# An mLSTM layer and a mixture of experts on one core: gate weights by another queue, all one-hot slot tables on VectorE, a wait before the second rank's weights, and a new order

## The chip, the cores and the metric

The kernel runs on one core of a Trainium2 chip. TensorE multiplies, VectorE, ScalarE and GpSimd work beside it, and SyncE issues most loads; every engine takes its instructions in the order in which the program was built and waits at the first whose inputs are not there. The metric is the device time of one launch in microseconds (us).

## The reference

Two layers follow each other. The first is a recurrence over 768 steps for 4 batches of 8 heads of 40 dimensions; the kernel computes it in closed form, row by row, as a numerator, a denominator and an output gate. The second sends each of the 3072 rows to the expert with the largest gate logit:

```python
h_tilde = np.einsum('bhde,bhe->bhd', C, qt)
y[:, :, t] = o * h_tilde / denom                  # first layer, x = y as 3072 rows of 320
logits = x @ w_gate
e_idx = np.argmax(logits, axis=1)
for e in range(E):                                # 8 experts
    h = np.maximum(x[e_idx == e] @ w1[e], 0.0)    # 320 -> 1024
    ye = h @ w2[e]                                # 1024 -> 320
    out[mask] = gate_w[mask, None] * eom[mask, e, None] * ye
```

## The kernel before, in words

**First stage.** The rows come in 24 tiles of 128, six per batch, worked in pairs n = 0 to 11 (three pairs per batch). For a pair, `hats_rows` (L1077) has TensorE make the numerators (L1007), ScalarE take the absolute denominator (L1095) and the sigmoid of the gate (L991), and VectorE multiply and divide (L1101, L1107, L1109). `logits_of` (L1164) transposes the rows (L1183, copies L1173), multiplies them with the gate weights `wg` (L488, L491), copies (L1195), transposes back (L1197) and adds (L1200). GpSimd then stores the pair to DRAM as part of `xn` (L1213).

**Routing.** Tiles are counted in five groups of 6, 6, 6, 4 and 2 (GROUPS, L35). `route` (L309) finds each row's expert and its place among the expert's rows, with VectorE and short products (L336 to L342). `invert` (L360) turns places into lists of row numbers: a one-hot table of slots `A`, 128 columns per tile, is multiplied with a table `T` (L388, L392, L398) and added to `acc` (L401). `A` is made in one of two ways: for a group in ONDVE (L50) by one VectorE compare over all its tiles (L373), else by two ScalarE activations per tile (L380, L382). Before, the groups of 4 and 2 tiles use VectorE, the three groups of 6 tiles use ScalarE.

**Early pair.** After groups 0 and 1 the busiest expert's first 256 rows among the first half are known. `early_gather` (L1228) has GpSimd fetch them in two indirect DMAs, after the row numbers `gi` (L414). `pair_products` (L694) transposes them (L741), splits them into a high and a low part (ScalarE L711, L713; VectorE L715, L717), multiplies with the expert's split first weights (64 products, L760), evacuates (L723, L725), and multiplies with its second weights (48 products, L776). The weights are split by L674 and L656. `first_gather` (L1240) and `first_columns` (L1251) fetch and transpose (L1272) the same expert's next 256 rows once all groups are known.

**Second stage.** The experts follow in order of size (rank 0 to 7): hidden products (L814, evacuated by L815 and L816), transposes of the next rank's rows (L788), result products (L841, evacuated by L849), scatters to the output (L679). `start` (L1397) issues the next rank's weight loads on SyncE's queue, `expert_load` (L583) and `gather` (L1401) its rows.

**What sets the order.** In the first stage no order stands in the code: the class `Play` (L100) holds each engine's clock, takes lines of work with weights and due times (tables at L41 to L78) and builds the instructions in the order that it finds; where TensorE would wait it puts in `fill` products (`warmup`, L1028), whose result nobody reads. SyncE's order is left to the framework.

Of the kernel before, what the change touches and what calls it, by code (L numbers as in the profile page):

```python
# [20 lines left out]
N, DM, E, F = B * S, H * D, 8, 1024  # L21
P = 128
# [15 lines left out]
GROUP1 = STARTS.index(TAKEN) - 1  # L38
TOP = 4096
TMAX = 32  # L40
WCHAIN, WSCALE, WPART, WPIECE, WEVAC, WGATE, WTOTAL, WLAST = -56800, 2000, -3800, -20600, 600, -12100, 3700, -30900  # L41
WSEND = -9800
WCAST, WGATHER, WSPLIT = 2000, -10000, -107800
AHATS, ALOGITS, AGATE = [-500, 21100, 8000, 3300, -11200, 12700, 3000, -11600, 10000, 11800, 9700, 3000], [600, -22800, -19800, -1600, -19600, -16300, -38600, 31500, -14300, -2800, -34800, 1200], [-11000, 11600, -11800, 10300, -5800, -1100, 13000, 14500, -8000, -1500, -2500, 12900]
AROUTED, ASEND, AREST = [4100, 0, 12300, 300, -1500], [-11800, -5300, -36700, 0, 0, 9900, 400, -8100, -15900, -7600, 22000, 19400], [6100, 3100, -3000, -7500, 5500, 900, 5800, -12000, 3000, -1100]
ASTATE, APAIRS = [27900, 3700, 300, 4100], [-800, -6000, -3300, 23700]
AKEYS = [0, 0, 0, 0]
AINV = [-400, -13500, -94300, -29100, -33500]
WSLOT, WINV, WFIRST = -1200, 1300, -10000
ONDVE = (3, 4)  # L50
STORE = 750
INVERTED = 3
QS = 1 << 12
WSTATE, WHATS, WLOGITS = -11900, -22200, -308100
SHORT = {'T': 1.0, 'V': 2.0, 'A': 3.0, 'G': 0.0}
AHEAD = 4
SCATTER = 1430
GATHERED = 2700
PERIOD, RISE, KEEP = 3413.3, 0.9, 0.7
FILL, SLACK, PART, NFILL = 120, 50, 0.85, 102  # L60
SEM = {"T": 52, "V": 35, "A": 36, "G": 200}
TAIL = {"T": 160, "V": 83, "A": 105, "G": 60}
LANDED = [
    ("small", (0, 14500, 21000, 27000)),
    ("queries", (9800, 18000, 24900, 32200, 13300)),
    ("load", (11000, 22300, 28300, 34700, 15400)),
]
SMALLS = (13500.0, 18500.0)
ROWS0 = 11500.0
WEIGHTS = (1400, 1400, 1350, 1800, 1800)  # L70
ISSUE, REACH, RINGFREE, MOVE = 1300, 1900, 30600, 1060
CLOCK = {"T": 9700.0, "V": 11500.0, "A": 10000.0, "G": 9200.0}
WPAIRS = -17800
WCHAIN1, WEARLY1 = -165400, 1550
SWITCH = 100
SEG = 8
FIRST = 3
WABS = -1700  # L78
FAR = 1 << 20
KW = [(0, 128), (128, 128), (256, 64)]  # L80
KL = [0, 128, 192]
# [127 lines left out]
def tile_mlstm_moe(  # L209
# [18 lines left out]
    nc = tc.nc  # L228
# [42 lines left out]
    wg = const.tile([P, 3, 32], F32, name="wg")  # L271
# [31 lines left out]
    def sync_after(inst, others):  # L303

        info = mybir.DependencyInfo(mybir.DependencyClass.Sync, mybir.DependencyReason.DATA)
        for o in others:
            tc.add_manual_dep(inst.ins, o.ins.name, info, reason="rows")
# [200 lines left out]
    G = rt.tile([BH, L0], F32, name="G")  # L508
# [71 lines left out]
        yield dve(8)  # L580
        nc.vector.tensor_copy(nr, ki)

    def expert_load(e_reg, twice=True):  # L583

        x = {}
        we = w1[bass.ds(e_reg, 1)].rearrange("a k f -> (a k) f")
        w2e = w2[bass.ds(e_reg, 1)].rearrange("a k f -> (a k) f")
        x["st1"], x["st2"] = [], []
        for kk in range(3):
            ws = wst.tile([P, F], F32, name="ws", bufs=3)  # L590
            if kk < 2:
                nc.sync.dma_start(ws, we[kk * P : (kk + 1) * P])
            else:
                for u in range(1 + twice):
                    nc.sync.dma_start(ws[64 * u : 64 * u + 64], we[256:320])
            x["st1"].append(ws)
        for u in range(2):
            ws = wst.tile([P, 4, DM], F32, name="ws2", bufs=2)
            nc.sync.dma_start(ws, w2e[u * 512 : (u + 1) * 512].rearrange("(c p) f -> p c f", p=P))
            x["st2"].append(ws)  # L600
        return x

    def expert_gather(pool, x, C, gi, src=xn, rows=N):

        n = (C + P - 1) // P
        x["ms"], x["C"] = [(j, min(P, C - j * P)) for j in range(n)], C
        width = src.shape[1]
        x["xg"] = xg = pool["xg"].tile([P, n, width], F32, name="xg")
        x["ids"] = gi if src is xn else xg[:, :, ID].bitcast(I32)
        for j, M in x["ms"]:  # L610
            yield "G", SCATTER
            nc.gpsimd.indirect_dma_start(  # L612
                out=xg[:, j, :] if src is xn else xg[:, j, :].bitcast(I32),
                out_offset=None,
                in_=src[:rows, :],
                in_offset=bass.IndirectOffsetOnAxis(ap=gi[:, j : j + 1], axis=0),
                bounds_check=rows - 1,
                oob_is_err=False,
            )
    def expert_weights(pool, x, cuts=1, rest=nc.vector):  # L620

        w1h = pool["w"].tile([P, 3, F], F32R, name="w1h")
        w1l = pool["w"].tile([P, 3, F], F32R, name="w1l")
        w2h = pool["w"].tile([P, F // P, DM], F32R, name="w2h")
        w2l = pool["w"].tile([P, F // P, DM], F32R, name="w2l")
        x["w"], x["parts"] = (w1h, w1l, w2h, w2l), 0
        for kk in range(3):
            for u in range(cuts):
                us = slice(u * F // cuts, (u + 1) * F // cuts)
                nc.scalar.copy(w1h[:, kk, us], x["st1"][kk][:, us])  # L630
                nc.vector.tensor_tensor(w1l[:, kk, us], x["st1"][kk][:, us], w1h[:, kk, us].bitcast(F32), ALU.subtract)  # L631
                x["parts"] += 1
                yield
        for u in range(2):
            for v in range(cuts):
                n = 4 // cuts
                vs = slice(v * n, v * n + n)
                us = slice(4 * u + v * n, 4 * u + v * n + n)
                nc.scalar.copy(w2h[:, us], x["st2"][u][:, vs])  # L639
                rest.tensor_tensor(w2l[:, us], x["st2"][u][:, vs], w2h[:, us].bitcast(F32), ALU.subtract)  # L640
                x["parts"] += 1
                yield
# [230 lines left out]
    with ExitStack() as actx:  # L873
# [53 lines left out]
        nc.scalar.dma_start(vab[:, 0:1], vp[:, 0:1])  # L927
        nc.scalar.dma_start(kt[L0:, 0:1], kn[:, 0:1, :DM])
        nc.scalar.dma_start(qkt[96:104, 0:1], qk0[96:104, 0:1])
        nc.sync.dma_start(kt[:L0, 0:1], kn[:, 0:1, :DM])  # L930
        lq = load_q(0, (L0, 2 * P, 4 * P, S))
        lo = load_o(0, (0, 2, 4, NCH))
# [101 lines left out]
        with tc.manual_schedule(engines=ENG):  # L1034
# [13 lines left out]
                eg.rearrange("p a b -> p (a b)")[:, L0:], G[:, L0 - 1 : L0].to_broadcast([BH, 2 * P - L0]), AF.Exp, scale=-1.0  # L1048
            )
            run(load_small(1))  # L1050
            nc.gpsimd.dma_start(wg[:, 0:2, : 2 * E], wgo[:, 0:2])
            nc.gpsimd.dma_start(wg[64:128, 2, : 2 * E], wgo[0:64, 2])
            wT_ps = psX.tile([P, BH], F32, name="wT_ps", tag="xt_ps")
            nc.tensor.transpose(wT_ps, wl.rearrange("p a b -> p (a b)"), ident[:BH, :BH])
            nc.vector.tensor_copy(wT, wT_ps)
# [18 lines left out]
            px, fx, apart, opened = {}, {}, [], []  # L1074
# [313 lines left out]
    with ExitStack() as mctx:  # L1388
# [5 lines left out]

        lt = mctx.enter_context(tc.tile_pool(name="lt", bufs=1))
        later = lt.tile([BH, 2, S - L0], F32, name="later")
        def start(r, x):  # L1397
            ev = nc.sync.value_load(er[0:1, r : r + 1], min_val=0, max_val=E - 1)
            x.update(expert_load(ev))

        def gather(r, x, gi=None):  # L1401
            if gi is None:
# [7 lines left out]
        with tc.manual_schedule(engines=ENG):  # L1410
            x, parts = {**fx, "w": px["w"]}, iter(())
            xs = {r: {"apart": apart} for r in range(1, E)}
            y = xs[1]
            start(1, y)
            run(gather(1, y, fx["next"]))
            for ob, j, M in px["leave"]:
                scatter(px, ob, j, M)
# [3 lines left out]
            for r in range(E):  # L1421
                if r + 1 < E:
                    y = xs[r + 1]
# [32 lines left out]
                x = y  # L1456
# [239 lines left out]
```

## Time and profile before

| | us |
|---|---|
| median of 3 runs | 278.29 |
| lowest, highest | 277.62, 279.69 |
| the profiled execution, its own time | 279.5 |
| its span | 277.7 |
| TensorE busy in the span | 264.1 (95%) |
| VectorE busy | 176.4 (64%) |
| ScalarE busy | 144.5 (52%) |
| GpSimd busy | 87.2 (31%) |

The profiled execution took 1.2 us more than the median of the runs. 1.8 us of its time lie outside its span. Busy time is an average over both stages; a stage is read from the windows, the timeline and the chain of waits.

### The profile page before, as it was taken

Reading aid. Unit: us, or ns where it says so; the run is one execution under the profiler, and the core shown is the slowest. Engines: PE = TensorE matmul, PEld = TensorE weight load, DVE = VectorE, ACT = ScalarE, POOL = GpSimd, SP = SyncE. Lnnn points to the kernel's source line nnn. Section 1 sums busy time; section 2 is a strip of 40 time slices with the busy share of each in tenths; the row PEclk is TensorE's granted clock in tenths of the full one; section 3 lists DMA queues with packets and bytes.
Section 4 is the critical chain, followed back from the end, with each engine's and each line's share of the span. In section 5 each row is a group of like instructions: output and inputs, shape, how many; then the busy total and the mean of one; then the engine's idle time right before and its main releaser. Section 6 shows DMA issues by size and latency. Waiting matters only on the chain.

```text
span 277.7 us, 5611 instructions
## 1 busy us (share of the span) xinstructions
PE 264.1 (95%) x2023; PEld 245.9 (89%) x2023; DVE 176.4 (64%) x526; ACT 144.5 (52%) x329; POOL 87.2 (31%) x109
## 2 busy tenths in 40 slices
PE   8979999899899999999999999999999999999990
PEld 5868888678789988999899989999999999899990
DVE  4544999799637986882885078608946955952300
ACT  4345677895517565633553266327626735732320
POOL 8251063353626116052403250323033231013021
PEclk9999999999999999999999999999999999999998
DMA  5999765971985587562555145524852761000000
GB/s 149 289 368 327 292 232 189 339 277 45 263 283 137 165 241 232 153 201 82 172 139 198 61 137 175 173 89 120 230 202 84 235 191 61 1 26 32 0 31 30
DMA packets 22355, 46.19 MB, mean 166 GB/s; under 512 B 2536, under 2 KB 15286, under 8 KB 22320
## 3 DMA queue, kind: packets, MB, share of 16 engines
q1 hardware_dynamic: 17856, 31.54, 36.9%
q0 software_dynamic: 4176, 14.04, 15.8%
q8 instruction: 18, 0.29, 0.4%
q10 hardware_dynamic: 288, 0.19, 0.3%
q14 instruction: 17, 0.14, 0.1%
HBM read 37.69 MB, written 8.42 MB: 166 GB/s over the span
## 4 chain that ended last, share of the span: by engine, by line
PE 53%; issue 17%; DMA 11%; DVE 8%; POOL 3%; SPq 2%; ACT 1%; POOLq 1%; DVEq 0%
PE hp L814 23%; PE op L841 22%; DMA xr<-in_on 7%; POOL out L679 3%; PE two L776 2%; DMA xg<-xn,gi 2%; PE xp L788 2%; DMA qTt<-in_qT 2%; SPq L912 1%; DVE xr L1101 1%; DVE w1l L656 1%; PE hat L1007 1%; POOLq L1455 1%; DVE xr L1109 1%; POOL xg L612 1%
## 5 line engine op out<-in xcount | busy, mean ns | idle before, releaser
L816 DVE SCALAR_TENSOR_TENSOR hl<-hp,hh 128x256 fp32r<-128x256 f32 (+6 forms) x64 | 35.6, 556 | 62.9 <-ACT hh L815 62.0
L679 POOL DMA_INDIRECT out<-ob,oi x28 | 31.6, 1127 | 117.4 <-ACT ob L849 101.5
L841 PE MATMUL op<-w2h,hh 128*128 128x320 f32 (+4 forms) x208 | 64.5, 311 | 0.0
L841 PE MATMUL op<-w2l,hh 128*128 128x320 f32 (+4 forms) x208 | 63.9, 308 | 0.0
L841 PE MATMUL op<-w2h,hl 128*128 128x320 f32 (+3 forms) x200 | 61.7, 309 | 0.0
L814 PE MATMUL hp<-xh,w1h 128*128 128x512 f32 (+6 forms) x168 | 58.0, 347 | 0.0
L814 PE MATMUL hp<-xh,w1l 128*128 128x512 f32 (+6 forms) x168 | 58.0, 347 | 0.0
L815 ACT ACTIVATE hh<-hp 128x256 fp32r<-128x256 f32 (+7 forms) x64 | 31.7, 495 | 33.4 <-PE hp L814 33.4
L814 PE MATMUL hp<-xl,w1h 128*128 128x512 f32 (+6 forms) x112 | 38.7, 346 | 0.0
L841 PEld LDWEIGHTS op<-w2h,hh 128*128 128x128 f32 (+4 forms) x208 | 37.9, 183 | 0.2
L612 POOL DMA_INDIRECT xg<-xn,gi x24 | 27.7, 1154 | 31.6 <-DVE w1l L631 9.2
L841 PEld LDWEIGHTS op<-w2l,hh 128*128 128x128 f32 (+4 forms) x208 | 37.5, 180 | 0.0
L841 PEld LDWEIGHTS op<-w2h,hl 128*128 128x128 f32 (+3 forms) x200 | 36.6, 183 | 0.0
L849 ACT ACTIVATE ob<-op,sc 128x320 f32<-128x320 f32 (+3 forms) x25 | 13.2, 526 | 43.7 <-PE op L841 43.7
L814 PEld LDWEIGHTS hp<-xh,w1l 128*128 128x128 f32 x168 | 31.6, 188 | 2.1
L814 PEld LDWEIGHTS hp<-xh,w1h 128*128 128x128 f32 x168 | 31.5, 188 | 2.0
L631 DVE TENSOR_TENSOR w1l<-ws,w1h 128x512 fp32r<-128x512 f32 x42 | 28.9, 687 | 0.0
L630 ACT CAST w1h<-ws 128x512 fp32r<-128x512 f32 x42 | 25.7, 613 | 0.0
L640 DVE TENSOR_TENSOR w2l<-ws,w2h 128x640 fp32r<-128x640 f32 x28 | 22.5, 823 | 0.9 <-ACT w2h L639 0.6
L814 PEld LDWEIGHTS hp<-xl,w1h 128*128 128x128 f32 x112 | 21.0, 188 | 1.4
L639 ACT CAST w2h<-ws 128x640 fp32r<-128x640 f32 x28 | 19.9, 716 | 0.0
L1007 PE MATMUL hat<-Cm,qTt 128*128 128x123 f32 (+3 forms) x144 | 18.9, 278 | 0.0
(238 smaller groups left out, 423.1 us busy)
## 6 DMA issues: line engine op xcount, KB each, us to landing
ws<-in_w SPq DMA_DIRECT2D x16, 640.0 KB, 4.9
ws<-in_w SPq DMA_DIRECT2D x16, 512.0 KB, 4.0
xn<-xr POOLq DMA_DIRECT2D x12, 336.0 KB, 3.7
ws<-in_w SPq DMA_DIRECT2D x15, 256.0 KB, 4.2
qTt<-in_qT SPq DMA_DIRECT2D x3, 1056.0 KB, 18.6
xr<-in_on SPq DMA_DIRECT2D x3, 960.0 KB, 17.5
xr<-in_on SPq DMA_DIRECT2D x3, 320.0 KB, 8.2
qTt<-in_qT SPq DMA_DIRECT2D x2, 384.0 KB, 8.7
```

The source lines that it names most:

```text
L612: nc.gpsimd.indirect_dma_start(out=xg[:, j, :] if src is xn else xg[:, j, :].bitcast(I32), out_offset=None, in_=src[:rows, :], in_offset=b ...
L630: nc.scalar.copy(w1h[:, kk, us], x["st1"][kk][:, us])
L631: nc.vector.tensor_tensor(w1l[:, kk, us], x["st1"][kk][:, us], w1h[:, kk, us].bitcast(F32), ALU.subtract)
L639: nc.scalar.copy(w2h[:, us], x["st2"][u][:, vs])
L640: rest.tensor_tensor(w2l[:, us], x["st2"][u][:, vs], w2h[:, us].bitcast(F32), ALU.subtract)
L679: i = nc.gpsimd.indirect_dma_start(out=out[:, :], out_offset=bass.IndirectOffsetOnAxis(ap=x["oi"][:M, j : j + 1], axis=0), in_=ob[:M, j, : ...
L814: nc.tensor.matmul(hp, a, c, start=(i == 0), stop=(i == len(mm) - 1))
L815: nc.scalar.activation(hh[:, f, :C], hp, AF.Relu)
L816: nc.vector.scalar_tensor_tensor(hl[:, f], hp[:, :C0], 0.0, hh[:, f, :C0].bitcast(F32), ALU.max, ALU.subtract)
L841: nc.tensor.matmul(op[:n], a, c, start=(i == 0), stop=(i == len(mm) - 1))
L849: nc.scalar.activation(ob[:M, j], op[:M], AF.Copy, scale=x["sc"][:M, j : j + 1])
L1007: nc.tensor.matmul(to, qTt[:, g, t0 : (c + 1) * P], Cm[b][:, cg], start=(g == 0), stop=(g == 2))
```

## The change

Four things are done, and the order tables are replaced by others:

1. The two loads of the gate weights `wg` go from GpSimd's queue (issued after the first batch's narrow loads) to ScalarE's queue at the start.
2. ONDVE holds all five groups: every one-hot table is one VectorE compare, of 768 columns for a group of 6 tiles, and the 36 ScalarE activations are gone.
3. The first weight load of the second rank waits for the two gathers of the first rank's rows (`after=fx["gathers"]`).
4. The narrow loads of batches 2 and 3 have later due times (SMALLS), with the landing times that `Play` reckons with, and its weights are new.

```diff
-WCHAIN, WSCALE, WPART, WPIECE, WEVAC, WGATE, WTOTAL, WLAST = -56800, 2000, -3800, -20600, 600, -12100, 3700, -30900
+WCHAIN, WSCALE, WPART, WPIECE, WEVAC, WGATE, WTOTAL, WLAST = -11600, 1500, -1800, -10100, -14800, -12700, 3700, -52300
...
-ONDVE = (3, 4)
+ONDVE = (0, 1, 2, 3, 4)
...
-GATHERED = 2700
+GATHERED = 3000
...
-    ("small", (0, 14500, 21000, 27000)),
+    ("small", (0, 14500, 22800, 30500)),
...
-SMALLS = (13500.0, 18500.0)
+SMALLS = (15500.0, 23500.0)
...
-    def expert_load(e_reg, twice=True):
+    def expert_load(e_reg, twice=True, after=()):
...
-                nc.sync.dma_start(ws, we[kk * P : (kk + 1) * P])
+                i = nc.sync.dma_start(ws, we[kk * P : (kk + 1) * P])
+                if after and not kk:
+                    sync_after(i, after)
...
-            nc.gpsimd.indirect_dma_start(
+            i = nc.gpsimd.indirect_dma_start(
...
+            x.setdefault("gathers", []).append(i)
...
+        nc.scalar.dma_start(wg[:, 0:2, : 2 * E], wgo[:, 0:2])
+        nc.scalar.dma_start(wg[64:128, 2, : 2 * E], wgo[0:64, 2])
...
-            nc.gpsimd.dma_start(wg[:, 0:2, : 2 * E], wgo[:, 0:2])
-            nc.gpsimd.dma_start(wg[64:128, 2, : 2 * E], wgo[0:64, 2])
...
-        def start(r, x):
+        def start(r, x, after=()):
...
-            x.update(expert_load(ev))
+            x.update(expert_load(ev, after=after))
...
-            start(1, y)
+            start(1, y, fx["gathers"])
```

The instruction rows below are the built programs'; the changed program's line numbers are higher by 2 from L593 on, by 3 from L620 on (L715 becomes L718), and by 5 between L930 and L1050.

ScalarE while groups 0 and 1 are inverted, before:

```order
L380 ACTIVATE far<-io_99,s_699 128x128
L1173 COPY xt<-xt_ps 128x3x128
L382 ACTIVATE A<-far 128x128
L1173 COPY xt<-xt_ps 128x3x128
L380 ACTIVATE far<-io_99,s_699 128x128
L382 ACTIVATE A<-far 128x128
L380 ACTIVATE far<-io_99,s_875 128x128
L1095 ACTIVATE dn<-hat 128x16
L382 ACTIVATE A<-far 128x128
L1195 COPY lt<-lg 128x128
```

and VectorE's rows for the same table of group 1 in the change:

```order
L364 TENSOR_SCALAR s_846<-rk 128x6
L367 SCALAR_TENSOR_TENSOR s_848<-s_846,rk 128x6
L388 TENSOR_TENSOR T<-block,s_846 128x192
L373 TENSOR_TENSOR A<-io_99,s_848 128x768
L502 COPY cnt<-ct 128x8
L392 TENSOR_TENSOR T<-T,number 128x192
```

ScalarE's slot activations stood between the copies (L1173, L1195) that the logits wait for; now VectorE has one wide compare instead.

VectorE ahead of the early pair's split (L715), before:

```order
L345 TENSOR_TENSOR t_1200<-pr,hots_135 128x16
L373 TENSOR_TENSOR A<-io_99,s_1190 128x512
L350 TENSOR_REDUCE rk<-t_1200 128x2
L392 TENSOR_TENSOR T<-T,number 128x128
L364 TENSOR_SCALAR s_1218<-rk 128x2
L656 TENSOR_TENSOR w1l<-ws,w1h 64x512
L367 SCALAR_TENSOR_TENSOR s_1230<-s_1218,rk 128x2
L502 COPY cnt<-ct 128x8
L388 TENSOR_TENSOR T<-block,s_1218 128x64
L572 TENSOR_TENSOR ns<-cnt,skip 128x8
L373 TENSOR_TENSOR A<-io_99,s_1230 128x256
L715 TENSOR_TENSOR xl<-two,xh 128x512
```

and in the change:

```order
L1203 TENSOR_REDUCE xr_216<-lg 128x2x16
L392 TENSOR_TENSOR T<-T,number 128x192
L315 TENSOR_REDUCE lmax<-xr_216 128x2
L323 TENSOR_REDUCE cm<-oh 128x4
L373 TENSOR_TENSOR A<-io_99,s_1073 128x768
L318 TENSOR_TENSOR oh<-xr_216,lmax 128x16
L326 TENSOR_TENSOR hots_134<-oh,cm 128x32
L437 TENSOR_REDUCE smax<-xg 128x2
L320 TENSOR_TENSOR oh<-oh,c_92 128x16
L718 TENSOR_TENSOR xl<-two,xh 128x512
L401 TENSOR_TENSOR acc<-acc,ix 128x32
```

The ranks and tables of the last two groups (4 and 2 tiles) stood ahead of the split, and stand behind it now.

TensorE where the first rank's rows are transposed (L1272), before, where 42 of the 48 of L776 stand behind the last row:

```order
L760 MATMUL two<-xh,w1l 128x256
L776 MATMUL two<-w2h,hh 128x320
L776 MATMUL two<-w2l,hh 128x320
L776 MATMUL two<-w2h,hl 128x320
L1272 MATMUL xp<-ident,xg 128x128 x2
L776 MATMUL two<-w2h,hh 128x320
L776 MATMUL two<-w2l,hh 128x320
L776 MATMUL two<-w2h,hl 128x320
L1272 MATMUL xp<-ident,xg 128x128 x2
```

and in the change, where 36 of L779 stand ahead of the first row:

```order
L779 MATMUL two<-w2h,hh 128x320
L779 MATMUL two<-w2l,hh 128x320
L779 MATMUL two<-w2h,hl 128x320
L1275 MATMUL xp<-ident,xg 128x128 x2
L779 MATMUL two<-w2h,hh 128x320
L779 MATMUL two<-w2l,hh 128x320
L779 MATMUL two<-w2h,hl 128x320
L1275 MATMUL xp<-ident,xg 128x128 x2
```

The transposes moved behind 39 of the 48 second products of the early pair, from behind 3 of them.

## Rows read from the trace of the kernel before

**Rows 1.** The page: engine, busy us, share of the span, instructions.
```profile
PE 264.1 (95%) x2023; PEld 245.9 (89%) x2023; DVE 176.4 (64%) x526; ACT 144.5 (52%) x329; POOL 87.2 (31%) x109
```
**Rows 2.** Windows of the second stage: length, busy time of each engine, clock, DMA.
```profile
100.00:150.00 50.00, 50.00 (x290) 45.88 (x289) 37.37 (x87) 26.46 (x53) 14.56 (x12) 1.00 0.56 170
200.00:250.00 50.00, 50.00 (x330) 49.27 (x329) 33.16 (x81) 26.99 (x58) 11.55 (x10) 1.00 0.37 116
```
**Rows 3.** The chain of waits: start, length, what; pieces from four places.
```profile
12.20 19.32 DMA xr<-in_on
...
67.23 6.09 DMA xg<-xn,gi
...
75.02 5.36 PE two L776 x36
...
82.33 6.89 PE hp L814 x56
```
**Rows 4.** Windows, VectorE alone: length, busy, instructions, clock, DMA share, GB/s.
```profile
25.47:62.99 37.52, 34.57 (x136) 1.00 0.77 269
50.00:53.40 3.40, 2.39 (x13) 1.00 1.02 331
20.00:25.47 5.47, 2.07 (x7) 1.00 1.03 311
```
**Rows 5.** Timeline of the handover: start, length, instruction, idle before and releaser.
```profile
62.32 0.67 DVE L715 TENSOR_TENSOR xl<-two,xh 128x512 fp32r<-128x512 f32 x1
...
62.92 0.17 DVE L401 TENSOR_TENSOR acc<-acc,ix 128x32 f32<-128x32 f32 x1
...
63.14 0.25 PE L398 MATMUL ix<-T,A 128*128 128x32 f16 x4 [0.19 <-DVE acc L401]
...
63.24 0.37 PE L760 MATMUL two<-xh,w1h 128*128 128x256 f32 x1
```
**Rows 6.** Groups of VectorE by form: busy us, mean ns, idle before.
```profile
L963 DVE TENSOR_TENSOR Pm<-sp,trif 128x256 f32<-128x256 f32 x4 | 1.7, 421 | 1.2 <-PE sp L958 1.2
...
L373 DVE TENSOR_TENSOR A<-io,s 128x512 f16<-128x512 f32 x1 | 0.7, 682 | 0.0
L373 DVE TENSOR_TENSOR A<-io,s 128x256 f16<-128x256 f32 x1 | 0.4, 409 | 0.0
L388 DVE TENSOR_TENSOR T<-block,s 128x128 f16<-128x128 int32 x1 | 0.3, 285 | 0.0
...
L320 DVE TENSOR_TENSOR oh<-oh,c 128x32 f32<-128x32 f32 x1 | 0.2, 182 | 0.0
```
**Rows 7.** Groups of ScalarE: the slot activations.
```profile
L380 ACT ACTIVATE far<-io,s 128x128 f32<-128x128 f32 x18 | 7.2, 400 | 0.0
L382 ACT ACTIVATE A<-far 128x128 f16<-128x128 f32 x18 | 5.6, 311 | 0.2
```
**Rows 8.** Timeline of the start: ScalarE's queue and first exponential, and TensorE's first logits.
```profile
2.35 0.72 ACTq L929 DMA_DIRECT2D qkt<-in_qk  x1
...
4.50 0.29 ACT L1045 ACTIVATE wl<-w 32x128 f32<-32x128 f32 x1
...
15.69 0.38 PE L488 MATMUL lg<-xt,wg 128*32 128x128 f32 x5 [1.75 <-DMA wg<-in_wgo]
```
**Rows 9.** Timeline of GpSimd: the early pair's gathers, the first rank's, the second's.
```profile
55.92 1.37 POOL L612 DMA_INDIRECT xg<-xn,gi  x1 [0.31 <-issue]
...
65.57 1.35 POOL L612 DMA_INDIRECT xg<-xn,gi  x1 [6.05 <-DVE ei L539]
67.23 1.03 POOL L612 DMA_INDIRECT xg<-xn,gi  x1 [0.30 <-DVE ki L579]
...
70.98 0.99 POOL L612 DMA_INDIRECT xg<-xn,next  x1 [0.31 <-issue]
```
**Rows 10.** Timeline of TensorE: three waits behind the start of the early pair.
```profile
67.72 0.39 PE L760 MATMUL two<-xh,w1h 128*128 128x256 f32 x1 [0.30 <-DVE hl L725]
...
73.37 0.33 PE L1272 MATMUL xp<-ident,xg 128*128 128x128 f32 x1 [1.02 <-DMA xg<-xn,gi]
...
82.33 0.39 PE L814 MATMUL hp<-fxh,w1h 128*128 128x256 f32 x1 [0.39 <-ACT ob L732]
```
**Rows 11.** All indirect gathers (L612), from issue to landing.
```profile
DMA to landing us min/median/max: 3.0/4.1/9.0
```
**Rows 12.** Timeline: the second rank's first weight loads, and their first cast.
```profile
67.79 0.96 SPq L592 DMA_DIRECT2D ws<-in_w  x2
...
86.35 0.61 ACT L630 CAST w1h<-ws 128x512 fp32r<-128x512 f32 x1
```

More of the change, by code (lines that the diff above doesn't have):

```diff
@@ L40 @@
 TMAX = 32
-WCHAIN, WSCALE, WPART, WPIECE, WEVAC, WGATE, WTOTAL, WLAST = -56800, 2000, -3800, -20600, 600, -12100, 3700, -30900
[L42 to L46, printed above, removed]
+WCHAIN, WSCALE, WPART, WPIECE, WEVAC, WGATE, WTOTAL, WLAST = -11600, 1500, -1800, -10100, -14800, -12700, 3700, -52300
+WSEND = -33700
+WCAST, WGATHER, WSPLIT = 2000, -69500, -16000
+AHATS, ALOGITS, AGATE = [10000, -2100, 8000, -1000, -5100, -15900, 300, 8600, 300, 500, 200, 0], [0, 300, 100, -42500, -5400, -4700, 0, -100, -600, 27200, 2900, -18600], [4100, -18600, 6500, -100, -16900, -10700, -4100, -3000, 4700, 15400, -4900, -8000]
+AROUTED, ASEND, AREST = [1800, -12000, -3100, -47400, -11000], [6000, 11000, 10500, 4100, -41200, 16700, 4900, 1200, 53800, -100, 0, 300], [-9500, 4200, -10700, 6000, -1000, -3100, 3000, 1900, -100, 300]
+ASTATE, APAIRS = [8000, 0, -5400, 11600], [21900, 300, -6400, 4700]
 AKEYS = [0, 0, 0, 0]
-AINV = [-400, -13500, -94300, -29100, -33500]
-WSLOT, WINV, WFIRST = -1200, 1300, -10000
-ONDVE = (3, 4)
+AINV = [-19200, -5200, 22600, -5900, -15500]
+WSLOT, WINV, WFIRST = -56100, -128600, -38000
+ONDVE = (0, 1, 2, 3, 4)
 STORE = 750
@@ L53 @@
 QS = 1 << 12
-WSTATE, WHATS, WLOGITS = -11900, -22200, -308100
+WSTATE, WHATS, WLOGITS = -41300, -22400, -328000
 SHORT = {'T': 1.0, 'V': 2.0, 'A': 3.0, 'G': 0.0}
@@ L63 @@
 LANDED = [
-    ("small", (0, 14500, 21000, 27000)),
-    ("queries", (9800, 18000, 24900, 32200, 13300)),
-    ("load", (11000, 22300, 28300, 34700, 15400)),
-]
-SMALLS = (13500.0, 18500.0)
-ROWS0 = 11500.0
+    ("small", (0, 14500, 22800, 30500)),
+    ("queries", (10400, 18500, 26000, 33000, 14300)),
+    ("load", (11900, 22900, 29700, 35500, 15900)),
+]
+SMALLS = (15500.0, 23500.0)
+ROWS0 = 11800.0
 WEIGHTS = (1400, 1400, 1350, 1800, 1800)
[L71 to L74, printed above, removed]
+ISSUE, REACH, RINGFREE, MOVE = 1300, 1900, 31800, 1060
+CLOCK = {"T": 10100.0, "V": 11700.0, "A": 10000.0, "G": 8200.0}
+WPAIRS = 2000
+WCHAIN1, WEARLY1 = -232000, 1550
 SWITCH = 100
@@ L77 @@
 FIRST = 3
-WABS = -1700
+WABS = -72900
 FAR = 1 << 20
```

## The prediction

> **What bounds the kernel now.** I read the page's totals first: TensorE is busy 95% of the span [rows 1]. The windows say where the other 5% can be: in the second stage TensorE is busy 50.00 of 50.00 us, twice [rows 2]. Nothing there can be won by this change, which leaves the second stage's products alone; a gain there would need fewer products. So the end comes a fixed stretch of TensorE work after the early pair's products begin (63.24 us [rows 5]), and the change is worth the shift of that moment, plus what is added to TensorE's work or waits behind it.
>
> What sets that moment is read backwards. The first product of the pair (L760) follows the last slot products (L398), which waited for VectorE's L401, and VectorE had just finished the split L715, at 62.99 [rows 5]. VectorE is the engine to look at: between the numerators of pair n = 3 (25.47) and the end of L715 it is busy 34.57 of 37.52 us, so it idles 2.95 us, 1.01 of them between 50.00 and 53.40 [rows 4]. Ahead of 25.47 it is busy only 2.07 of 5.47 us [rows 4], because the loads are not there: the chain of waits passes through one that takes 19.32 us [rows 3].
>
> **The slot tables.** ScalarE loses 18 pairs of activations of 0.400 and 0.311 us, 12.8 us in all [rows 7]. VectorE gains three compares of 768 columns, which the trace does not show. Their price is bounded by 0.68 us (the 512-column compare) and twice that, 1.36; the rows for 256 and 512 columns, 0.409 and 0.682, differ by 0.273, so I take 0.955 each, 2.9 us together [rows 6].
>
> **The new order of VectorE.** Counted from the same point (numerators of n = 3) to L715, the program before has 135 instructions, the change 117. Behind L715 go the two narrower compares (0.68 and 0.41), a table step of 0.285, a mask of 0.421 (this one ahead of n = 3) and some 17 small steps of the last groups' ranks near 0.18 to 0.2 [rows 6]: about 5.1 us. In come the 2.9 us, and one small step. Net −2.1 us of durations. But an instruction starts before its predecessor's record ends: L715 runs to 62.99 and L401 starts at 62.92 [rows 5]. With 0.07 us for each of 18 instructions fewer, 1.2 us of it is no gain. I take **−0.9 us** (bounds −2.1 and 0).
>
> **VectorE's idle time.** It can fall because ScalarE no longer puts 12.8 us of slot work between the copies that the logits need. It need not vanish, since logits still make round trips through TensorE. I take half, **−1.5 us** (bounds 0 and −2.95). The start of the stretch, 25.47, I leave where it is: it hangs on loads whose bytes are the same. Spacing the narrow loads can move it by some tenths either way.
>
> **The gate weights.** Two more issues on ScalarE, each bounded by 0 and about 0.72 (the last one there took 0.72), push the first exponential from 4.50 to about 5.9 [rows 8]. What hides it: VectorE's 3.4 idle us between 20 and 25.47 [rows 4]. On the other side TensorE waited 1.75 us for these weights, until 15.69 [rows 8]; that ends in the same idle time. Both count nothing. If the loads came earlier, the 1.4 us would show.
>
> **The handover.** In the change L760 stands behind L401 and seven more rank products, so I add 0.25 us between L715 and the pair. The pair then starts at 63.24 − 0.9 − 1.5 + 0.25 = **61.1, 2.15 us earlier**.
>
> **Behind the start.** The ranks of the last group, the counts and the slot products of the last two groups, 22 small products, are now inside the pair, two of them before as well. Four took 0.25 us with their wait [rows 5]; 20 cost between 0.4 and 1.2, I take **+0.65**. TensorE's waits there were 0.30 + 1.02 + 0.39 = 1.71 us [rows 10]. In the change I count them again. VectorE has 37 instructions between L715 and the first rank's row numbers, 10.7 us of durations less 37 × 0.07, so these are there about 7.6 us after the pair starts. The second gather is issued 1.66 us after the first [rows 9], and lands 4.1 us later by the median of all gathers [rows 11], 6.1 in this place before [rows 3]: 13.4 to 15.4 us after the start. TensorE arrives at the transposes L1272 after 64 products of 0.123, 0.65 of small ones, and 39 of 0.149 [rows 3], at 14.3. So the wait is 0 to 1.1 us. Behind it only nine second products are left as cover for the splits of these rows, where there were 45; I allow 0.4. And VectorE's weight remainders arrive about as TensorE wants them; I allow 0.3. Together 1.2 us, **−0.5** against 1.71.
>
> **The second rank's weights.** Their first load was issued at 67.79, their first cast ran at 86.35 [rows 12]. The new order alone puts the sorted experts later, the wait puts the loads behind a gather that lands near 74.5 to 76.5. Their cover is the time up to the cast, at about 84.3: 8 to 10 us for a load of 512 KB. I cost the wait at nothing. If that cover were gone, the cast would stand in front of the hidden rows' evacuations on ScalarE, and every us of it would reach TensorE. What it gives: the rows before landed 6.1 us after their issue, against a median of 4.1 [rows 3, 11], beside these loads.
>
> **A rule against the change.** GpSimd's gathers took 1.35 and 1.37 us to issue where VectorE was full, and 0.99 at 70.98 [rows 9]. So a fuller VectorE costs a gather 0.4 us, in front of the early pair 0.8 for two, which it can wait for: the rows of the pair should be there about 1 us before VectorE comes to L715. [...]
>
> **Sum.** −2.15 + 0.65 − 0.5 = −2.0 us. The profiled execution took 279.5, so it would take 277.5; it lies 1.2 above the median of 278.29, and against that the forecast is **276.3 us**.
>
> **Rivals.**
> - *VectorE runs dense* (0.22). All 2.95 us of idle go: the pair starts at 59.6. Then −3.6 + 0.65 − 0.5 = −3.5, 274.8 us. For it: ScalarE is nearly half freed. Against: the last pairs' logits hang on each other through three engines.
> - *The idle time stays* (0.20). Then the waits were round trips and not ScalarE; −0.65 + 0.65 − 0.5, so 277.8 us, no change. This is also what comes out if the wide compares only move the work from one full engine to a fuller one.
> - *The first rank's rows come too late* (0.10). Before, 45 second products stood behind the first of their transposes, now nine. From a landing later than about 5 us after issue TensorE stands still, in full. At the largest landing seen, 9.0 [rows 11], it waits 4.0 us, and the splits that were hidden add about 0.9 (a cast and a subtraction). With the idle staying as well: −0.65 + 0.65 + 4.0 + 0.9 − 1.7 = +3.2, 281.5 us, slower; with the forecast's gain, 280.0. For it: 6.1 us in this very place. Against: the weight loads that shared the time now wait.
>
> **The numbers.** The forecast itself has 0.48, with its own range from 275.4 to 277.4. The range that holds the time 8 times in 10 takes in the dense case's centre and the unchanged one's scatter: 274.3 to 279.0. About 1%, 2.8 us, is what a measurement can tell here. Faster by more than that is below 275.5: most of the dense case and a tail of the forecast, 0.28. Slower by more is above 281.1: most of the late rows, 0.07. The rest, 0.65, is within 1%.
>
> **What would show it.** In the profile after: the first L763 near 61 us; VectorE's idle time between the numerators of n = 3 and L718 about 1.5 us; one wide compare of 0.95 us; the wait before the first L1275 under 1.1 us; the second rank's weights issued near 75 and no wait of ScalarE before their cast; the second stage as full as before. The prediction is wrong if the pair starts no earlier than 63, if the loads make the numerators of n = 3 or n = 6 late, if L1275 waits for several us, or if the granted clock, 1.00 in the windows before [rows 2, 4], falls somewhere because 60 fill products stand where there were 78.

## The result and the profile after

| | before | changed |
|---|---|---|
| median, 4 runs each (us) | 278.98 | 274.52 |
| lowest, highest | 277.62, 279.69 | 274.24, 275.19 |
| the profiled execution: own time, span | 279.5, 277.7 | 275.19, 273.4 |
| TensorE busy in the span | 264.1 | 260.7 |

The ratio is 0.985, with a 95% interval from 0.980 to 0.990. The kernel is 1.5% faster here; when it ran again, in two of the sets below, the ratio was 0.994 and 0.995. A ratio and its interval go by the fast runs alone, those within 1.5% of a kernel's fastest, while a median is of all its runs. The profiled execution lost 4.3 us where the sum said 2.0. By the sum's own terms:

| term (us) | predicted | in the two traces |
|---|---|---|
| start of the stretch (numerators of n = 3) | 0 | 25.47 to 24.62: −0.85 |
| VectorE busy, from there to the end of the split | −0.9 | 34.57 to 31.64: −2.93 |
| VectorE idle in it | −1.5 | 2.95 to 2.06: −0.89 |
| handover, split's end to the pair | +0.25 | 0.25 to 0.33: +0.08 |
| start of the early pair | −2.15 | 63.24 to 58.65: −4.59 |
| all behind that start | +0.15 | 214.5 to 214.7: +0.2 |

VectorE in windows of the changed kernel (window, length, busy with instructions, clock, DMA share, GB/s), which answer to [rows 4]:

```profile
24.62:58.32 33.70, 31.64 (x119) 1.00 0.86 289
20.00:24.62 4.62, 1.73 (x7) 1.00 1.05 391
```

The second row says that the idle time ahead of n = 3 is still there. The first is where the gain lies: 3.8 us less, 2.9 of them work. The handover (start, length, instruction, idle before it and what ended it), to be laid beside [rows 5]:

```profile
57.65 0.67 DVE L718 TENSOR_TENSOR xl<-two,xh 128x512 fp32r<-128x512 f32 x1
58.25 0.17 DVE L401 TENSOR_TENSOR acc<-acc,ix 128x32 f32<-128x32 f32 x1
...
58.47 0.18 PE L336 MATMUL pr<-qbase,ones 128*128 128x32 bf16 x1 [0.19 <-DVE acc L401]
...
58.65 0.36 PE L763 MATMUL two<-xh,w1h 128*128 128x256 f32 x1
```

TensorE follows L401 with a wait of 0.19 us, as before. What bounds the start of the pair is still VectorE. The wide compare, by groups of VectorE (count, busy, mean ns):

```profile
L373 DVE TENSOR_TENSOR A<-io,s 128x768 f16<-128x768 f32 x3 | 2.8, 945 | 0.0
```

0.945 us against the 0.955 read off the two narrower ones [rows 6]. Next the start, ScalarE's queue and engine, then TensorE's first logits, beside [rows 8]:

```profile
3.10 1.28 ACT L901 ACT_TABLE_LOAD   x1 [3.10 <-issue]
3.66 0.40 ACTq L933 DMA_DIRECT2D wg<-in_wgo  x1
4.10 0.48 ACTq L934 DMA_DIRECT2D wg<-in_wgo  x1
...
4.63 0.31 ACT L1050 ACTIVATE wl<-w 32x128 f32<-32x128 f32 x1
...
13.62 0.41 PE L488 MATMUL lg<-xt,wg 128*32 128x128 f32 x4 [0.72 <-ACT xt L1176]
```

The two issues took 0.40 and 0.48 us, 0.68 of it while the engine loaded its table (3.10 to 4.38). The first exponential moved from 4.50 to 4.63, not to 5.9. TensorE no longer waits for the gate weights. TensorE's waits from the small products to 100 us (total, times, longest), which answer to [rows 10]:

```profile
PE hp L817 <- DVE fxh L1267: 0.5, 1, 0.5
PE two L779 <- ACT ob L735: 0.4, 1, 0.4
PE ix L398 <- DVE A L373: 0.3, 1, 0.3
PE pr L336 <- DVE acc L401: 0.2, 1, 0.2
```

The last two stand ahead of the pair. The transposes L1275 are not in the list, so the first rank's rows were there: 0.9 us of waits behind the start, against 1.71 before and 1.2 foreseen. GpSimd's gathers of these rows, TensorE's transposes, and the second rank's weights (issue and first cast), to [rows 9, 12]:

```profile
66.77 1.09 POOL L614 DMA_INDIRECT xg<-xn,gi  x1 [8.95 <-DVE gi L414]
68.16 1.47 POOL L614 DMA_INDIRECT xg<-xn,gi  x1 [0.30 <-DVE ei L539]
...
73.28 0.38 PE L1275 MATMUL xp<-ident,xg 128*128 128x128 f32 x2
```
```profile
72.24 0.97 SPq L592 DMA_DIRECT2D ws<-in_w  x2
...
81.55 0.61 ACT L633 CAST w1h<-ws 128x512 fp32r<-128x512 f32 x1
```

The cast has no wait in its row, so the cover of 9.3 us held. In the second stage TensorE is as full as in [rows 2] (window, length, then busy time of TensorE, its weight loads, VectorE, ScalarE, GpSimd, then clock, DMA share, GB/s):

```profile
100.00:150.00 50.00, 50.00 (x301) 46.68 (x300) 33.48 (x81) 24.54 (x48) 17.35 (x14) 1.00 0.54 167
200.00:250.00 50.00, 50.00 (x331) 49.26 (x330) 29.54 (x66) 25.84 (x55) 11.64 (x11) 1.00 0.34 105
```

**Where the 2.0 us of busy time come from that the sum had not.** Compared by line and shape, VectorE's durations between n = 3 and the split fell by 4.1 us, of which the overlap of 17 instructions fewer takes back 1.1: the deduction of 0.07 us each was right. What left and what came makes −2.3, near the −2.1 predicted. The other 1.8 us are in steps that both programs have there, 1.3 of them in L364, L367, L543 and L556, eight short steps. Before, five of them ran long (start, length), each beside GpSimd; four meetings from the timeline of the kernel before:

```profile
38.08 0.73 POOL L970 TENSOR_TENSOR vw<-vab,vw 128x320 f32<-128x320 f32 x1
38.12 0.72 DVE L367 SCALAR_TENSOR_TENSOR s<-s,rk 128x6 f32<-128x6 int32 x1
...
42.09 0.72 POOL L1213 DMA_DIRECT2D xn<-xr  x1 [1.42 <-DVE ei L539]
42.40 0.39 DVE L543 TENSOR_SCALAR erf<-erf 128x8 f32<-128x8 f32 x1
...
46.95 0.94 POOL L652 MEMSET w1l<- 64x1024 f32 x1
47.58 0.35 DVE L556 TENSOR_SCALAR skip<-cnt 128x8 f32<-128x8 f32 x1
...
54.50 1.11 POOL L612 DMA_INDIRECT xg<-xn,gi  x1 [0.76 <-DVE xr L1200]
55.22 0.37 DVE L364 TENSOR_SCALAR s<-rk 128x6 int32<-128x6 int32 x1
```

Each VectorE row ends within 0.04 us of the GpSimd row above it. Away from GpSimd's rows such a step takes 0.16 to 0.17 in this trace (L364 at 45.80, L367 at 45.99). In all four GpSimd had begun first; why VectorE's step then ends with it, no row shows. In the changed kernel none of the eight ran long, in any of its three traces; in two more traces with the order of before, four of them did, by 0.7 and 0.9 us in all. A meeting alone is not enough: in the changed kernel L543 took 0.17 us at 36.55, amid GpSimd's DMA issue of 36.34 to 37.05. It went the other way once, with VectorE first: 0.73 us for a GpSimd product that took 0.22 in the trace before (at 37.78), where it costs nothing:

```profile
36.92 0.82 DVE L1112 TENSOR_TENSOR xr<-xr,dn 128x640 f32<-128x640 f32 x1
37.07 0.73 POOL L974 TENSOR_TENSOR vw<-half,egT 128x8 f32<-128x8 f32 x1
```

### The profile page after: what moved, and what is told of

Read it like the earlier page. It is cut to its first block, busy times and chain, and to the rows that moved or that the text cites. A ratio compares the mean times of both kernels' runs of the same rounds, so it can differ in the third digit from the quotient of the medians.

```text
span 273.4 us, 5551 instructions
## 1 busy us (share of the span) xinstructions
PE 260.7 (95%) x2005; PEld 243.2 (89%) x2005; DVE 176.6 (65%) x529; ACT 134.9 (49%) x293; POOL 87.1 (32%) x107
## 4 chain that ended last, share of the span: by engine, by line
PE 81%; DMA 5%; issue 5%; DVE 4%; POOL 1%; ACT 1%; SPq 0%; POOLq 0%; ACTq 0%
PE hp L817 31%; PE op L844 30%; PE hat L1012 4%; DMA xr<-in_on 4%; PE two L763 3%; PE xp L791 3%; PE two L779 3%; PE xt_ps L1186 2%; DMA qTt<-in_qT 2%; POOL out L682 1%; PE lg L488 1%; DVE xr L1104 1%; DVE xr L1112 1%; PE st L987 1%; PE hat L1007 1%
## 5 line engine op out<-in xcount | busy, mean ns | idle before, releaser
L682 POOL DMA_INDIRECT out<-ob,oi x28 | 31.6, 1129 | 110.4 <-ACT ob L852 100.9
L818 ACT ACTIVATE hh<-hp 128x256 fp32r<-128x256 f32 (+7 forms) x64 | 31.7, 495 | 34.1 <-PE hp L817 34.1
L614 POOL DMA_INDIRECT xg<-xn,gi x24 | 29.0, 1207 | 32.9 <-DVE hl L819 9.8
L852 ACT ACTIVATE ob<-op,sc 128x320 f32<-128x320 f32 (+3 forms) x25 | 13.2, 526 | 43.8 <-PE op L844 43.8
L817 PEld LDWEIGHTS hp<-xh,w1l 128*128 128x128 f32 x168 | 31.6, 188 | 2.1
L817 PEld LDWEIGHTS hp<-xh,w1h 128*128 128x128 f32 x168 | 31.6, 188 | 2.0
```

The source lines that it names most:

```text
L614: i = nc.gpsimd.indirect_dma_start(out=xg[:, j, :] if src is xn else xg[:, j, :].bitcast(I32), out_offset=None, in_=src[:rows, :], in_offs ...
L682: i = nc.gpsimd.indirect_dma_start(out=out[:, :], out_offset=bass.IndirectOffsetOnAxis(ap=x["oi"][:M, j : j + 1], axis=0), in_=ob[:M, j, : ...
L817: nc.tensor.matmul(hp, a, c, start=(i == 0), stop=(i == len(mm) - 1))
L818: nc.scalar.activation(hh[:, f, :C], hp, AF.Relu)
L852: nc.scalar.activation(ob[:M, j], op[:M], AF.Copy, scale=x["sc"][:M, j : j + 1])
```

## Experiments

They ran in three sets, the first eight on one chip, the last four on another. In both the kernel before took more time than above (medians 282.15, 282.15 and 282.39), and the traces hold fewer landing records of DMAs (2,017 to 2,120, against 2,339 before and 2,337 after). So they are read by stretches, each from its own trace (us). Each edit of ONDVE or of the due times also makes the planner find another order, so no run moves the one-hot tables alone:

| kernel | n = 3 | VectorE busy, idle to the split's end | pair starts | pair to first result product | from there to the end | median, ratio to before (95%) |
|---|---|---|---|---|---|---|
| before, first trace | 25.47 | 34.6, 2.95 | 63.24 | 27.1 | 187.4 | |
| before, again | 24.59 | 34.4, 5.6 | 64.84 | 27.3 | 187.8 | |
| changed, first trace | 24.62 | 31.6, 2.1 | 58.65 | 26.9 | 187.8 | 274.52, 0.985 |
| changed, second | 24.37 | 31.6, 2.4 | 58.70 | 34.3 | 187.1 | 282.24, 0.994 (0.988 to 1.000) |
| changed, third | 24.08 | 31.6, 2.5 | 58.51 | 34.2 | 187.0 | 283.35, 0.995 (0.991 to 0.999) |
| gate weights on the old queue | 25.96 | 31.7, 2.8 | 60.77 | 35.3 | 188.0 | 282.99, 1.005 (1.001 to 1.008) |
| no weights' wait | 24.30 | 31.6, 2.4 | 58.65 | 33.9 | 187.4 | 282.06, 1.001 (0.998 to 1.004) |
| order only | 24.27 | 31.7, 2.0 | 58.33 | 33.2 | 188.1 | 281.98, 1.000 (0.997 to 1.003) |
| longer weights' wait | 23.24 | 31.6, 2.6 | 57.81 | 34.4 | 187.4 | 282.33, 1.002 (0.999 to 1.005) |
| group 0 on ScalarE | 24.04 | 31.5, 4.2 | 59.96 | 32.8 | 187.7 | 284.47, 1.005 (1.001 to 1.010) |
| new order, slots on ScalarE | 26.06 | 33.6, 5.2 | 65.11 | 27.1 | 187.4 | 281.75, 0.996 (0.992 to 0.999) |
| narrow loads early | 23.89 | 36.5, 2.8 | 63.40 | 25.6 | 188.1 | 278.85, 0.988 (0.985 to 0.991) |
| before, gate weights only | 26.27 | 34.5, 5.5 | 66.48 | 27.1 | 187.5 | 281.04, 0.997 (0.994 to 0.999) |
| before, all tables on VectorE only | 26.10 | 38.5, 3.2 | 67.81 | 30.5 | 186.9 | 286.98, 1.017 (1.014 to 1.021) |

Some of these traces are disturbed ahead of the pair as well. In before again, TensorE's semaphore for a logits product that ended at 54.2 came 1.8 us late. ScalarE and then VectorE waited for it, where the same rows of the first trace show waits of at most 0.2 us:

```profile
56.05 0.27 ACT L1195 COPY lt<-lg 128x128 f32<-128x128 f32 x1 [1.94 <-PE fill L1031]
56.74 0.22 DVE L1200 TENSOR_REDUCE xr<-lg 128x32 f32<-128x64 f32 x1 [1.69 <-PE lg L1197]
59.06 0.23 DVE L1200 TENSOR_REDUCE xr<-lg 128x32 f32<-128x64 f32 x1 [0.77 <-PE lg L1197]
```

TensorE stood for 1.8 us meanwhile, and its granted clock was 0.50 from 57.0 to 60.4. So about 2.5 us of this trace's 5.6 idle are not the order's. Before, gate weights only has the same late product at 55.8 and the clock of 0.50 from 58.3 to 61.8; all tables on VectorE only has one 1.3 us late at 58.4 and that clock from 15.0 to 18.4; group 0 on ScalarE has one 0.8 us late at 51.7. A fair measure of the change is the stretch from n = 3 to the pair: 37.8 us in before's first trace, also in its second less those 2.5, and 34.0, 34.3 and 34.4 in the changed kernel's three.

**Gate weights on the old queue.**

```diff
-        nc.scalar.dma_start(wg[:, 0:2, : 2 * E], wgo[:, 0:2])
+            nc.gpsimd.dma_start(wg[:, 0:2, : 2 * E], wgo[:, 0:2])     # after load_small(1), both loads
```

> The changed kernel with the gate weights loaded by GpSimd's queue again, after the first batch's narrow loads; the order on the engines is the same. Theory A (the early gate weights opened the start): in the changed kernel group 0's first maximum ran at 23.81 us against 27.32 before, so about 1.0 us of VectorE's routing moved ahead of the numerators of n = 3 and these began 0.85 us earlier. Undoing it then costs 1.9 us: 276.4, the first logits wait until about 15.7, and the early pair starts near 60.5 instead of 58.6. Theory B (the forecast's: these weights' wait ends in idle time): under 0.5 us slower, and the pair starts at 58.6 to 59.0.

The pair began 2.1 us later, as theory A said, but not for its reason. The first logits ran at 15.88 and had waited 0.24 us for a copy, not for the weights. What was late is TensorE's clock. The first clock record of a trace is one of 1.00, and a window ahead of it reads 1.00 only because it has no record: there `fill` products of 244 columns follow each other every 0.20 us, behind it every 0.11, so TensorE ran at little over half its later pace until then, and the clock rose there. The rise came at 13.0 us in this trace, at 13.2 and 14.0 in the new order with slots on ScalarE and in before, gate weights only, where the gate weights come early, and at 3.8 to 9.3 in the other eleven. The run that follows has the weights on the old queue and an early rise (3.8).

**Order only**: the kernel before with the change's tables, ONDVE and due times, and neither the gate weights' move nor the wait.

> The kernel before with the changed kernel's tables (all one-hot tables on VectorE, spaced narrow loads, new order), but with the gate weights on GpSimd's queue and without the weights' wait. Theory A (the order and VectorE's freed time are the whole gain): within 0.3% of the changed kernel. Rival (the early gate weights are worth 1.9 us of the gain): 0.7% slower than the changed kernel, the pair starts near 60.5, and the numerators of n = 3 are late.

The pair starts at 58.33, as in the changed kernel, so theory A holds for this stretch: the gate weights' move is not where the 4.6 us come from. TensorE waited 1.82 us for them, until 14.52, and n = 3 still stood at 24.27: this wait ends in idle time, as forecast. VectorE in that trace's window:

```profile
24.27:58.00 33.73, 31.69 (x119) 1.00 0.88 292
```

**Before, gate weights only**: the two loads moved, nothing else.

> The kernel before, with only the gate weights' two loads moved to ScalarE's queue at the start; the order on the engines is that of before. Theory A (the early gate weights opened the start): TensorE's wait of 1.75 us for them goes, the numerators of n = 3 come 0.5 to 1.5 us earlier than 25.47, and the time falls by as much: 276.8 to 277.8 against 278.3. Theory B (that wait ended in idle time): within 0.3 us of before, the numerators of n = 3 at 25.2 to 25.7 because the rows' load sets them.

0.35% faster than before (0.06 to 0.65%): about theory A's size, and the interval comes down to theory B. Its trace had the late rise of the clock (n = 3 at 26.27) and cannot settle it. With the order-only run, which shows none of it ahead of the pair, the early gate weights are worth between nothing and about 1 us.

**No weights' wait.**

```diff
-            start(1, y, fx["gathers"])
+            start(1, y)
```

> The changed kernel, with the second rank's first weight load no longer waiting for the first rank's gathers; the order on the engines is the same. Theory A (the wait costs and gives nothing here, since 39 second products stand ahead of the transposes): within 0.3 us of the changed kernel, loads issued near 68, gathers landing up to 2 us later and still in time. Rival: the weights share the queues with the gathers, the rows land 6 us or more after their issue as before, and the transposes wait 0.5 to 1.5 us: 275.0 to 276.0.

Up to the transposes its trace is the changed kernel's: pair at 58.65, transposes at 73.28. The loads left at 71.13 instead of 72.24, since SyncE got the sorted experts only at 70.6 in either. So the wait held the loads back by 1.1 us, where some 4 had been expected, and that is worth nothing here: theory A, on a weaker test than planned.

**Before, all tables on VectorE only.**

```diff
-ONDVE = (3, 4)
+ONDVE = (0, 1, 2, 3, 4)
```

> The kernel before, with only all five groups' one-hot tables on VectorE; the order that the planner finds with the old tables differs. Theory A (VectorE's load ahead of the split decides): three compares of 0.95 us come in ahead of the split and nothing leaves, so the pair starts 2.9 us later less at most the 2.95 us of idle time: 0 to 2.9 us slower, 278.3 to 281.2. Rival (ScalarE's slot work was what held VectorE up): the idle time goes as well and the time is within 0.5 us of before or below.

1.7% slower, and the pair at 67.81. VectorE's busy time grew by 3.9 us in its window, and of the idle time 3.2 us were left, some 0.7 of them from the late product named above:

```profile
26.10:67.75 41.65, 38.49 (x150) 1.00 0.69 232
```

Freed ScalarE alone brings nothing. The order that the planner finds with its old settings holds all five tables ahead of the split.

**New order, slots on ScalarE**: the changed kernel with ONDVE = (3, 4).

> The changed kernel with groups 0 to 2's one-hot tables made by ScalarE again, as before; gate weights, wait and weights of the planner as in the change. The planner then puts the last two groups' tables ahead of the split L718 again: 134 VectorE instructions from the numerators of n = 3 to L718, against 117 in the change. Theory A (what gave the gain is that the last groups' ranks and tables stand behind the split): these 17 instructions, 5.1 us less 0.07 each, come in and three compares of 0.945 go, so +1.1 us, and the idle time is that of before or more: the pair starts at 60 to 62 instead of 58.7. Rival (the weights of the planner and ScalarE's order gave it, wherever the tables are made): the pair starts at 59.2 or earlier.

The pair starts at 65.11, beyond theory A's 60 to 62: about 1.9 us of that are the late rise of the clock, busy time is up by 2.0, and idle time by 2.8 against the changed kernel's second trace, which is more than foreseen:

```profile
26.06:64.91 38.85, 33.62 (x136) 1.00 0.74 244
```

**Narrow loads early.**

```diff
-    ("small", (0, 14500, 22800, 30500)),
+    ("small", (0, 14500, 21000, 27000)),
-SMALLS = (15500.0, 23500.0)
+SMALLS = (13500.0, 18500.0)
```

> The changed kernel with the old due times of the narrow loads. The planner then finds another order: all five one-hot tables ahead of the split, 136 VectorE instructions instead of 117. Theory A (the place of the last groups decides): the 19 more cost 5.1 us less 0.07 each and some waits, and the pair starts at 62 to 63.5 instead of 58.7, the kernel is 1 to 2% slower than the changed one in the same company. Rival (the due times matter through the loads alone): the numerators of n = 3 move by less than 0.5 us and the pair starts at 58.3 to 59.5.

The pair starts at 63.40, as theory A says: 138 VectorE instructions in the window instead of 119, and 4.9 us more busy time.

```profile
23.89:63.20 39.31, 36.48 (x138) 1.00 0.79 265
```

n = 3 moved by 0.2 to 0.7 us only (23.89), so the due time matters because the planner tips over into another order. But the time went against the expectation: in its set this was the fastest kernel, 1.2% faster than before, for what happens behind the pair, told below.

**Group 0 on ScalarE**: ONDVE = (1, 2, 3, 4).

> The changed kernel with group 0's one-hot table made by ScalarE again (12 activations, 4.3 us), groups 1 to 4 on VectorE. Theory A (VectorE's load ahead of the split decides): one compare of 0.95 us leaves VectorE, ScalarE has room, and the pair starts 0.5 to 0.95 us earlier than 58.6: 0.2 to 0.35% faster than the changed kernel. Rival (ScalarE's slot work between the logits' copies is what costs): VectorE idles more by as much as it saves, the pair starts at 58.6 or later, and the time is the changed kernel's or up to 1.5 us more.

The rival holds. A compare left VectorE, and the pair still came 1.3 us later: against the changed kernel's second trace, VectorE's waits for the logits (L1203) and ahead of the numerators' product (L1104) grew from 1.5 to 3.2 us; up to 0.3 of that, in the wait at 53.35, may be the late product at 51.7. It shows the other half of the forecast: ScalarE's slot work does cost idle time on VectorE.

**The changed kernel, and the kernel before, again.**

> The changed kernel itself, in the company of the others. In the run without the weights' wait ScalarE's first evacuation of the hidden products (L818) came at 81.40 instead of 77.93, and TensorE stood still for 3.5 us at 82 and then had half the clock for some 7 us. Theory A (the wait before the second rank's weights prevents this): the changed kernel shows no such stall, its first L818 is near 78, and it is 1.2 to 2% faster than before. Theory B (the stall is this chip's or this moment's, whatever the kernel's wait): the first L818 is late here too, by 2 to 4 us, and the gain is under 0.7%.

> The kernel before itself, for its trace on the same chip as the others. By both theories the pair (L760) starts near 63.2 as in the first trace. If TensorE stands still somewhere that it did not in the first trace, or has a lower clock for a stretch, then that belongs to the chip and not to the edits, and only the stretch up to the pair's start is to be compared.

> The changed kernel once more, as the measure for the others of this call. By both theories the pair starts at 58.7; where the stretch from the first hidden product to the first result product takes 9 us as in its first trace, the kernel is 1.2 to 2% faster than before; where it takes 15 to 16 us as in its second trace, the 6 us won ahead of the pair are given back and the difference is under 0.7%.

The start of the pair came again, 58.70 and 58.51: 4.5 and 4.7 us ahead of before's first trace, 6.1 and 6.3 ahead of its second, of which about 2.5 are that trace's disturbance. But the gain was given back: from the pair to the first result product the changed kernel took 34.3 us instead of 26.9, and every kernel with its order 32.8 to 35.3. In the second trace, ScalarE's first evacuations of hidden products, and TensorE in two windows:

```profile
83.67 0.38 ACT L818 ACTIVATE hh<-hp 128x256 fp32r<-128x256 f32 x1 [5.32 <-remote]
86.42 0.66 ACT L818 ACTIVATE hh<-hp 128x256 fp32r<-128x256 f32 x2 [2.37 <-remote]
```
```profile
70.00:80.00 10.00, 8.57 (x59) 7.64 (x58) 3.43 (x20) 2.05 (x5) 6.08 (x7) 1.00 0.72 207
80.00:90.00 10.00, 5.53 (x34) 5.11 (x34) 3.27 (x16) 3.06 (x10) 3.98 (x4) 0.87 0.86 272
```

In the first trace the same evacuation ran at 77.93. Here its product was issued at 77.56, and the semaphore record that released ScalarE stands at 83.52; the next product ended at 79.6, and ScalarE ran for it at 86.42. TensorE ran on until it had to wait for a tile that ScalarE and VectorE free (3.40 us, until 87.32), and then had a granted clock of 0.50 from 87.5 to 90.9 (0.87 in the mean of that window). In the first two traces no semaphore was late by over 0.6 us.

**Longer weights' wait.**

```diff
-            start(1, y, fx["gathers"])
             run(gather(1, y, fx["next"]))
+            start(1, y, y["gathers"])
```

> The changed kernel, with the second rank's first weight load waiting for that rank's own four gathers (landed near 83.5) instead of for the first rank's two (landed near 72). Theory A (the wait is free only as long as its cover lasts): the loads are issued 11 us later, their first cast comes at 88 to 89 instead of 81.6, and stands in front of evacuations on ScalarE: the time from the first hidden product to the first result product grows from 9.0 by 4 to 7 us, the whole kernel by as much. Rival (ScalarE has room and the weights are wanted only for the second rank's products): under 1.5 us. Rival on the disturbance seen in the changed kernel's second trace (semaphores 2 to 4 us late between 77 and 86, when weights, gathers and products of the first rank meet): with the weights out of that stretch, the late semaphores go and ScalarE's first L818 is at 78 again.

The weights were issued 6.2 us later (78.40), not 11, because the gathers were in by then, so they did not leave that stretch. ScalarE's first L818 came at 78.57, as the rival on the disturbance said, and its second only at 85.12, for a product that had ended at 77.9. So the run does not decide whether the weights have a part in it:

```profile
78.57 0.38 ACT L818 ACTIVATE hh<-hp 128x256 fp32r<-128x256 f32 x1 [2.73 <-PE hp L817]
85.12 0.38 ACT L818 ACTIVATE hh<-hp 128x256 fp32r<-128x256 f32 x1 [6.17 <-remote]
```

With TensorE standing anyway, this run can't tell what the cover is worth; that part stays open. What goes with the longest delays in these twelve traces is GpSimd's row of indirect DMAs. In the changed order ten follow each other 0.3 us apart, from 72.0 to 85.3 in its first trace, and there no semaphore was late, so the row alone does not do it; in the later traces that order had delays of 4 to 7 us. In the order before they stand in two pieces, and the delays reached 2.7 us; this is its trace from the second set:

```profile
75.19 1.00 POOL L612 DMA_INDIRECT xg<-xn,next  x1 [0.30 <-issue]
83.03 1.03 POOL L679 DMA_INDIRECT out<-ob,oi  x1 [6.84 <-ACT ob L732]
```

With narrow loads early there are gaps as well (2.4 and 1.6 us before the two scatters), its semaphores were late by up to 2.5 us, and its stretch to the first result product took 25.6 us. That order also has second products between the first hidden ones (78.40 to 80.27); whether these or the gaps spared it was not tested. Why increments come late on these two chips, and whether they would without a profile, stays open.

## Why the prediction was right, and where it was wrong

- **What bounds it**: right. The end moved with the start of the pair (−4.6 and −4.3), and the work behind it stayed within 0.2 us.
- **The slot tables and the new order**: the direction was right, and the runs show that it needs both parts: all tables on VectorE with the planner's old settings is 1.7% slower, and its new settings with slots on ScalarE, or with the last groups ahead of the split, start the pair at 63 us or later. The size failed here: −0.9 for the new order of VectorE, where −2.93 was measured. The count of instructions, the compares and the overlap came out nearly as written. What the step took for granted is that the steps which both programs share cost the same in both: they got 1.8 us shorter, 1.3 of it in the eight of which five had run long beside GpSimd.
- **The start of the stretch**: it was to stay, because "it hangs on loads", and it moved by −0.85. In the first trace of before it did hang on its load: that of the gate L991, issued at 6.96, landed at 24.48 by the trace's landing records (the load of 19.32 us in [rows 3] lands at 31.52 and is a later pair's). The gate ran at 24.70, behind copies in ScalarE's queue that ended at 24.67:

```profile
23.33 0.86 ACT L1173 COPY xt<-xt_ps 128x384 f32<-128x384 f32 x2 [0.31 <-PE xt_ps L1183]
...
24.21 0.46 ACT L1153 COPY kt<-kt 64x320 f32<-64x320 f32 x1
24.70 1.36 ACT L991 ACTIVATE xr<-xr 128x640 f32<-128x640 f32 x2
```

  In the changed order the gate stands ahead of such copies, and runs when its load lands, at 22.91:

```profile
22.93 0.74 ACT L996 ACTIVATE xr<-xr 128x640 f32<-128x640 f32 x1 [0.87 <-DMA xr<-in_on]
```

  But the −0.85 cannot be put down to the change. In the second trace of before the same load landed at 22.22, 2.3 us earlier than in the first, the copies held the gate until 23.82, and n = 3 stands at 24.59, where the changed kernel has it:

```profile
23.34 0.46 ACT L1153 COPY kt<-kt 64x320 f32<-64x320 f32 x1
23.82 1.36 ACT L991 ACTIVATE xr<-xr 128x640 f32<-128x640 f32 x2
```

  So between two traces of one kernel the load's landing moves by 2.3 us and n = 3 by 0.9, and that part of the gain may be luck. Ahead of the same n = 3, the changed order also does group 0's first routing steps, where VectorE idled before.
- **The idle time**: half of it was to go, 0.9 of 2.95 went. The rival that it vanishes gave 274.8, next to the time measured, but 2.06 us are still idle: a right time for a wrong reason.
- **The gate weights**: nothing on the sum, and the runs leave between nothing and about 1 us. The issues took 0.88 us and not 1.4, and 0.68 of that was hidden beside the table load rather than by VectorE's idle time.
- **Behind the start**: +0.15 against +0.2. The first rows landed 3.1 us after their issue, the second by 72.1, 4 us after theirs; their transposes did not wait, and the weights' wait cost nothing.
- **The rule against the change**: a fuller VectorE was to cost a gather 0.4 us, and the runs do not show it. The early pair's two gathers took 1.11 and 1.46 us to issue, against 1.11 and 1.37 before, with VectorE busy through the whole of both in the changed kernel; and in the kernel before VectorE was just as busy through the 0.99 us of the gather at 70.98. None of the three wide compares (at 32.60, 43.08 and 56.44) met a gather.
- **The chances**: 0.65 lay on a time within 1% of before, and the kernel is faster by 1.5%. The time is at the low edge of the range, because the start of the stretch (−0.85) and the shared steps (−1.8) stood at zero in the sum. The rows of those steps could have been read; how late that load would land could not.

## What to carry to other kernels

When a stretch is bound by one engine, look at every group whose mean is above that of its shape elsewhere: the excess may come from what another engine runs beside it (here 0.72 us for an L367 beside GpSimd, 0.17 elsewhere), and another order can remove it or bring it back. A gain ahead of a handover must be followed to the end; here late semaphores in the stretch behind it gave back more than was won, on two chips and for a cause that stays open. Compare such kernels by stretches, and on more than one chip, before a difference of 1% is believed.

## What the runs showed of the hardware

- Four VectorE steps of 0.16 to 0.17 us took 0.35 to 0.72 in the trace before, where they began while GpSimd ran a memset, a product or a DMA issue, and ended within 0.04 us of it; one beside a DMA issue in the changed kernel did not (0.17 at 36.55). With VectorE first, GpSimd's 0.22 us product took 0.73 there (at 37.07).
- TensorE's clock first rose between 3.8 us (order only) and 14.0 us (before, gate weights only); `fill` products followed each other every 0.20 us ahead of the rise and every 0.11 behind it. Where it came at 13.0 to 14.0, n = 3 stands at 25.96 to 26.27, against 23.24 to 25.47 in the ten traces whose rise was earlier and whose clock did not fall before n = 3.
- TensorE's semaphore increments came 1 to 7 us after products that ended between 75 and 97 us in all twelve later traces, and 0.8 to 1.8 us late between 51 and 59 us in four of them; in the first two none was late by over 0.6 us.
